# A new order of issue for the first nine slots of a sparse attention with a folded feed-forward

## The chip, the cores and the metric

One NeuronCore of a Trainium2 chip. The metric is the device time of one execution in microseconds; before the change three runs gave a median of 270.12 us (268.2 to 274.05).

## The reference

```python
# q, k, v: (8, 8, 576, 64) float32
rel = pos[:, None] - pos[None, :]
mask_local   = (rel >= 0) & (rel < 32)                      # heads 0 to 3
mask_strided = (rel >= 0) & (pos[None, :] % 32 == pos[:, None] % 32)   # heads 4 to 7
scores = np.where(masks, q @ k.T / sqrt(64), -1e9)
attn = softmax(scores) @ v
x = attn.transpose(0, 2, 1, 3).reshape(4608, 512)
# feed-forward: w1, w2 (512, 1024), w3 (1024, 1024), w_out (1024, 512)
out = ((x @ w1) * (x @ w2)) @ w3 @ w_out
```

## The kernel before, in words

The heads are taken two at a time. A "pair" i is one batch element and two heads: there are 32 pairs, four to a batch element, of which the first two (i % 4 of 0 and 1) have the local mask and the other two the strided one. The sparse masks let scores be computed in small blocks: nine 64-wide blocks for a local pair, eleven residue groups of 54 for a strided one.

The steps of a pair, each a helper of its own:

- `load_qk` and `load_v`: q and k come through POOL's DMA queue and are converted to 16 bit on the way. v of a strided pair does so too, in four transfers (L130); v of a local pair comes in 32 bit through SP's queue (L117, L119).
- `emit_cast_v`, `shift_v`: for a local pair, v is converted on a compute engine (L281) and a copy that is shifted by 32 rows is made by two DMAs of SP's queue (L289, L290).
- `emit_T`: q and k are transposed on PE (L301) into PSUM, and copied out (L309 on ACT or DVE for local pairs, L314 on DVE and L315 on ACT for strided ones). There are two PSUM buffers of this kind, shared with `emit_P`.
- `emit_S`: the scores on PE (L333 local, L339 strided) and on DVE the addition of the mask (L345).
- `emit_max`, `emit_sub` on DVE (L353, L360), `emit_exp` on ACT (L372).
- `emit_norm`: sum and reciprocal on DVE (L380, L382), and the multiplication (L383) on POOL or, where the call says so, on DVE.
- `emit_P`: the weights are transposed on PE (L401) and copied out (L404).
- `emit_V`: the products with v on PE (L421 local, L438 strided), copied into the four xT tiles.

In parallel w3 and w_out are folded into one 1024 x 512 matrix, wfh. w3 is loaded in four quarters (`load_w3(c, 2)` with c = 0, 2, 4, 6 brings rows c and c + 1), w_out in two halves (`load_wo`). `fold_t(mc)` transposes one of eight row blocks of w3 on PE (L223, copied out by L225), and `fold_m(mc, half)` multiplies it with half of w_out (four matmuls of L233; the second half ends with a copy, L236). w1 and w2 come in two halves each (`load_w`, L205).

The feed-forward is a row of pieces, handed out by `feed(us, batches)`: it emits pieces until their costs (0.87 us for an x @ w1 or x @ w2 piece, four matmuls of L248 or L258; 1.74 for an output piece, L269) have used up the credit given. Six PSUM buffers are shared by scores, folds, products with v and the feed-forward.

The order on each engine is the order in which these helpers are called. For slots 0 to 8 the calls are written out by hand, and from slot 9 on a loop issues them in a regular pattern. Engines wait for each other by semaphores that the framework sets from the data and the buffers. Every queue is in order, so a transfer that stands behind a waiting POOL instruction waits with it. In the built program a DMA of POOL waits on one of eight counters, which the DMA eight places before it used too.

Of the kernel before, what the change touches and what calls it, by code (L numbers as in the profile page):

```python
# [27 lines left out]
def kernel(  # L28
# [11 lines left out]
    nc = tc.nc  # L40
# [47 lines left out]
    def load_qk(i, which="qk"):  # L88

        b, hp, local, par = where(i)  # L90
        h0 = 2 * hp
        t = cast.get(i)
        if t is None:
            t = cast[i] = ld.tile([P, 2, ST * D], FP16, tag="s16", bufs=4, name="s16")
        if i + 1 == 4 * B:
            for p0 in (0, HALF):
                nc.vector.memset(t[p0 + 32:p0 + HALF, 1, (ST - 1) * D:ST * D], 0.0)
        for src, p0 in [((q, 0), (k, HALF))["qk".index(c)] for c in which]:
            if local:
                nc.gpsimd.dma_start(t[p0:p0 + HALF, :, 0:LB * D],  # L100
                                    src[b, h0:h0 + 2].rearrange("h (p j) d -> p h (j d)", j=LB))
            else:
                for h in range(2):
                    for r0, ap, n in strided_rows(i, h, ST):
                        nc.gpsimd.dma_start(t[p0 + r0[0]:p0 + r0[1], h, 0:n * D],  # L105
                                            _ap(src[b, h0 + h], 0 + ap[0], ap[1] + [[1, n * D]]))
# [100 lines left out]
    def load_wo(c):  # L207
        nc.gpsimd.dma_start(woh[:, c:c + 4, :], wor[:, c:c + 4, :])

    def load_w3(c, n=2):  # L210
        w3 = wst.tile([P, n, DF], FP16, tag="w3s", bufs=4, name="w3s")
        nc.gpsimd.dma_start(w3.rearrange("p i n -> p (i n)"), w3r[:, c // 2, :])
        for i in range(n):
            w3st[c + i] = w3[:, i, :]
# [62 lines left out]
    def emit_cast_v(i, eng=nc.gpsimd.tensor_copy):  # L277
        b, hp, local, par = where(i)
        if local:
            vst = staged.pop(i)  # L280
            eng(out=vhL[par][:, 1], in_=vst)  # L281
            pts.setdefault(i, {})["v"] = vhL[par]
# [208 lines left out]
    def zero_S():  # L491
        for t in qTS + prS:
            nc.vector.memset(t, 0.0)

    def zero_L(i):
        nc.vector.memset(kTL[i][:, 0:QB], 0.0)
        nc.vector.memset(vsL[i][HALF:P, LC - 1], 0.0)
        nc.vector.memset(vhL[i][0:QB, 0, 0], 0.0)
        nc.vector.memset(prL[i][:, LB, :], 0.0)

    dve = nc.vector
    cp, act, pool = nc.vector.tensor_copy, nc.scalar.copy, nc.gpsimd.tensor_copy
    with tc.manual_schedule():
        zero_S()
        load_qk(1, "q")
        zero_L(1)
        load_qk(0, "q")
        load_qk(1, "k")
        load_v(1)
        load_qk(0, "k")  # L510
        load_qk(2, "k")
        emit_cast_v(1, cp)
        load_w3(2, 2)
        make_identity(nc, id16)
        make_maskL()
        zero_L(0)
        load_qk(2, "q")
        emit_T(0)
        load_w3(4, 2)
        emit_T(1)  # L520
        make_sel()
        load_wo(0)
        make_maskS()
        emit_S(0)
        load_qk(3, "q")
        fold_t(2, act)
        emit_max(0)
        emit_sub(0)
        emit_S(1)
        load_qk(3, "k")  # L530
        emit_T(2)
        emit_exp(0)
        fold_t(3, act)
        load_wo(4)
        load_v(0, True)
        fold_t(4, act)
        emit_max(1)
        fold_t(5, cp)
        emit_S(2)
        fold_m(5, 0)  # L540
        load_v(2)
        fold_m(3, 0)
        emit_sub(1)
        emit_exp(1)
        emit_norm(0, dve)
        load_w3(6, 2)
        load_qk(4, "k")
        fold_m(4, 0)
        load_qk(4, "q")
        emit_max(2)  # L550
        load_qk(5, "k")
        emit_norm(1)
        fold_m(2, 0)
        emit_T(3)
        emit_sub(2)
        emit_S(3)
        load_qk(5, "q")
        emit_max(3)
        fold_m(5, 1)
        fold_m(4, 1, cp)  # L560
        emit_exp(2)
        fold_m(3, 1, cp)
        emit_sub(3)
        emit_P(1, cp)
        fold_m(2, 1)
        fold_t(6, act)
        load_w3(0, 2)
        fold_t(7, cp)
        emit_T(4, cp)
        emit_exp(3)  # L570
        emit_norm(2, dve)
        fold_m(6, 0)
        emit_S(4)
        emit_max(4)
        emit_cast_v(0, act)
        load_qk(6, "q")
        emit_sub(4)
        load_qk(6, "k")
        emit_T(5)
        fold_m(7, 0)  # L580
        fold_m(7, 1)
        emit_P(2)
        emit_P(0, cp)
        load_qk(7, "k")
        load_w(w1r, w1h, 0)
        emit_S(5)
        load_qk(7, "q")
        fold_t(0, act)
        fold_t(1, cp)
        emit_T(6)  # L590
        load_v(3)
        emit_max(5)
        load_w(w2r, w2h, 0)
        fold_m(1, 0)
        emit_norm(3)
        shift_v(0)
        emit_exp(4)
        emit_sub(5)
        emit_exp(5)
        fold_m(1, 1, cp)  # L600
        fold_m(0, 0)
        emit_norm(4)
        fold_m(6, 1)
        emit_P(3)
        shift_v(1)
        load_w(w1r, w1h, 1)
        fold_m(0, 1)
        emit_V(0)
        emit_norm(5)
        emit_S(6)  # L610
        emit_T(7)
        emit_max(6)
        emit_V(1)
        emit_V(2)
        load_w(w2r, w2h, 1)
        emit_V(3)
        load_v(4, True)
        emit_P(4)
        emit_P(5)
        emit_sub(6)  # L620
        load_v(5, True)
        emit_exp(6)
        emit_S(7)
        feed(0.65, 1)
        feed(1.67, 1)
        emit_max(7)
        emit_norm(6)
        feed(0.54, 1)
        load_qk(8, "q")
        load_qk(8, "k")  # L630
        feed(0.90, 1)
        feed(2.64, 1)
        emit_P(6, cp)
        feed(0.53, 1)
        feed(1.52, 1)
        emit_cast_v(4, act)
        shift_v(4)
        load_qk(9, "q")
        load_v(6)
        emit_cast_v(5, act)  # L640
        feed(0.11, 1)
        shift_v(5)
        emit_sub(7)
        load_qk(9, "k")
        emit_exp(7)
        emit_norm(7, dve)
        feed(1.96, 1)
        feed(0.98, 1)
        load_v(7)
        load_qk(11, "q")  # L650
        emit_T(8)
        feed(0.65, 1)
        feed(0.65, 1)
        load_v(8)
        load_qk(10, "q")
        load_v(9, True)
        load_qk(13, "k")
        feed(0.65, 1)
        emit_S(8)
        emit_V(4, cp)  # L660
        emit_cast_v(8, act)
        feed(0.30, 1)
        emit_T(9, cp)
        load_qk(10, "k")
        load_v(10)
        emit_V(5, cp)
        emit_V(6)
        load_qk(12, "q")
        feed(0.65, 1)
        shift_v(8)  # L670
        emit_max(8)
        load_qk(11, "k")
        emit_sub(8)
        feed(1.34, 1)
        emit_exp(8)
        emit_norm(8)
        load_qk(13, "q")
        emit_P(7)
        feed(1.33, 1)
        emit_cast_v(9, cp)  # L680
        load_qk(12, "k")
        feed(0.20, 1)
        feed(1.58, 1)
        for n in range(9, NP + 2):
            full = (n - 1) // 4
            first = full - 1 if n % 4 == 1 else full
            f = 5.2
            if n < NP:
                shift_v(n)
                emit_S(n)  # L690
            if n + 1 < NP:
                emit_T(n + 1)
            if n + 5 < NP:
                load_qk(n + 5)
            for i in (n + 3, n + 2):
                if i < NP and where(i)[2] == (i == n + 3):
                    load_v(i)
            for i in (n - 3, n - 2):
                if i + (3 if by_dma(i) and i % 4 < 3 else 2) == n:
                    emit_V(i)  # L700
            if n < NP:
                emit_max(n)
            feed(0.1 * f, first)
            if n < NP:
                emit_sub(n)
                emit_exp(n)
                emit_norm(n)
                if n + 1 < NP:
                    emit_cast_v(n + 1)
            feed(0.15 * f, first)  # L710
            if n <= NP and not by_dma(n - 1):
                emit_P(n - 1)
            feed(0.55 * f, full)
            if n < NP and n % 2 == 1:
                for i in (n - 1, n):
                    if by_dma(i):
                        emit_P(i)
            feed(0.2 * f, full)
        feed(1e9, B)
# [31 lines left out]
```

## Time and profile before

| | |
|---|---|
| median of three runs | 270.12 us (268.2, 274.05, 270.12) |
| the profiled execution | 271.13 us, span 269.4 us |
| PE busy | 251.3 us, 93% of the span |
| DVE, ACT, POOL busy | 176.0, 140.7, 152.8 us |
| DMA | 38.75 MB, mean 144 GB/s |
| first transpose of q and k (L301) | 6.53 us |
| first matmul of the fold (L233) | 19.14 us |
| first feed-forward product (L248) | 46.50 us |

The span runs from the first to the last instruction of the core; the execution's own time is 1.7 us longer. Where PE's busy share is near 100% the time is set by PE; elsewhere the row "idle before" of an instruction and its releaser tell what PE waited for. DMA rates count the bytes as they were written, in 16 bit for what was converted on the way.

### The profile page before, as it was taken

To read this page: it belongs to the slowest core of one execution; us is meant where nothing else is said; L and a number is where in the kernel's file an instruction comes from. 1 tells how busy PE (TensorE), PEld (TensorE's weight loads), DVE (VectorE), ACT (ScalarE), POOL (GpSimd) and SP (SyncE) were. 2 spreads that over 40 slices of the span, in tenths; PEclk is the share of its full clock that TensorE was granted. 3 is DMA by queue.
4 is the path that set the end of the run, shared out by engine and by line. 5 is a ranking of instruction groups with operands and counts; after the bars stand their busy time and mean duration, and the time that the engine had idled before them with its cause. 6 is when DMAs were issued, how large, how long until landed. Compare 5 with 4: busy or idle time off the path is not lost. (4 is left out here: it accounts for less than half of the span.)

```text
span 269.4 us, 9826 instructions
## 1 busy us (share of the span) xinstructions
PE 251.3 (93%) x4186; PEld 131.2 (49%) x4186; DVE 176.0 (65%) x353; ACT 140.7 (52%) x256; POOL 152.8 (57%) x236
## 2 busy tenths in 40 slices
PE   0588997999999999999999999999999999999995
PEld 0464655445554555554555455544454444444443
DVE  2379997677778777868886787678768823432210
ACT  1563767565754664666566456545655444333322
POOL 8757776398984895489568846885684110000000
PEclk9999999999999999999999999999999999999999
DMA  7999999999999699699999997996688142001113
GB/s 118 192 198 208 185 198 147 174 162 205 225 199 186 107 227 202 98 193 176 175 110 228 190 144 70 259 179 97 52 210 102 30 105 82 2 0 76 42 58 141
DMA packets 66238, 38.75 MB, mean 144 GB/s; under 512 B 45589, under 2 KB 60945, under 8 KB 66193
## 3 DMA queue, kind: packets, MB, share of 16 engines
q0 software_dynamic: 22112, 17.29, 43.0%
q1 hardware_dynamic: 44080, 20.82, 37.8%
q8 instruction: 33, 0.54, 0.8%
q14 instruction: 13, 0.10, 0.1%
HBM read 39.24 MB, written 9.44 MB: 181 GB/s over the span
## 5 line engine op out<-in xcount | busy, mean ns | idle before, releaser
L248 PE MATMUL aps<-xT,w1h 128*128 128x512 f16 x288 | 74.1, 380 | 0.0
L258 PE MATMUL bps<-xT,w2h 128*128 128x512 f16 x288 | 73.9, 379 | 0.0
L261 DVE TENSOR_TENSOR abt<-bps,asb 128x512 f16<-128x512 f32 x72 | 47.7, 678 | 33.1 <-PE bps L258 29.6
L269 PE MATMUL ops<-wfh,abt 128*128 128x512 f16 (+1 forms) x296 | 65.6, 374 | 0.0
L252 ACT COPY asb<-aps 128x512 f32<-128x512 f32 x72 | 41.4, 586 | 33.3 <-PE aps L248 20.2
L258 PEld LDWEIGHTS <-w2h 128*128 128x128 f16 x288 | 28.2, 98 | 34.0
L130 POOL DMA_DIRECT2D vhS<-in_v_dram x70 | 42.5, 719 | 3.8 <-DMA woh<-in_moe_w_out_dram 2.2
L269 PEld LDWEIGHTS <-abt 128*128 128x128 f16 x296 | 27.8, 98 | 30.3
L248 PEld LDWEIGHTS <-w1h 128*128 128x128 f16 x288 | 27.0, 98 | 30.7
L383 POOL TENSOR_TENSOR prS<-prS,rc 128x594 f16<-128x594 f16 x14 | 16.8, 1202 | 38.0 <-DVE rc L382 16.0
L274 ACT COPY osb<-ops 128x512 f32<-128x512 f32 (+1 forms) x36 | 20.7, 578 | 29.2 <-PE ops L269 24.2
L360 DVE TENSOR_TENSOR tmp<-tmp,mx 128x576 f32<-128x576 f32 (+1 forms) x32 | 25.7, 804 | 0.9
L353 DVE TENSOR_REDUCE mx<-tmp 128x9 f32<-128x576 f32 (+1 forms) x32 | 24.2, 758 | 0.5
L105 POOL DMA_DIRECT2D s<-in_q_dram x35 | 21.0, 631 | 6.0 <-PE tpk L301 2.1
L301 PE MATMUL tpq<-id,s 54*64 54x54 f16 (+1 forms) x640 | 17.6, 196 | 7.2 <-DMA s<-in_q_dram 6.5
L105 POOL DMA_DIRECT2D s<-in_k_dram x35 | 21.6, 679 | 2.0 <-DMA s<-in_q_dram 1.6
L372 ACT ACTIVATE prS<-tmp 128x594 f16<-128x594 f32 x16 | 11.2, 702 | 19.6 <-DVE tmp L360 12.4
L383 POOL TENSOR_TENSOR prL<-prL,rc 128x576 f16<-128x576 f16 x15 | 18.4, 1224 | 5.4 <-ACT osb L274 4.0
L301 PEld LDWEIGHTS <-s 54*64 54x64 f16 (+1 forms) x1280 | 14.7, 111 | 11.6 <-DMA s<-in_q_dram 6.5
L301 PE MATMUL tpk<-id,s 54*64 54x54 f16 (+1 forms) x640 | 17.4, 196 | 2.3 <-DMA s<-in_k_dram 2.0
L380 DVE TENSOR_REDUCE sm<-prS 128x11 f32<-128x594 f16 x16 | 12.3, 770 | 10.6 <-ACT prS L372 10.6
L380 DVE TENSOR_REDUCE sm<-prL 128x9 f32<-128x576 f16 x16 | 12.0, 749 | 10.9 <-ACT prL L372 10.9
(78 smaller groups left out, 271.5 us busy)
## 6 DMA issues: line engine op xcount, KB each, us to landing
out_dram<-osb SPq DMA_DIRECT2D x35, 256.0 KB, 2.8
vsL<-in_v_dram SPq DMA_DIRECT2D x32, 128.0 KB, 5.2
s<-in_q_dram POOLq DMA_DIRECT2D x16, 144.0 KB, 4.3
s<-in_k_dram POOLq DMA_DIRECT2D x16, 144.0 KB
s<-in_k_dram POOLq DMA_DIRECT2D x31, 74.2 KB, 5.1
s<-in_q_dram POOLq DMA_DIRECT2D x31, 74.2 KB, 5.7
w3s<-in_moe_w_dram POOLq DMA_DIRECT2D x4, 512.0 KB, 7.0
vhL<-vhL SPq DMA_DIRECT2D x16, 120.0 KB, 4.6
```

The costliest lines, as they stand in the source:

```text
L105: nc.gpsimd.dma_start(t[p0 + r0[0]:p0 + r0[1], h, 0:n * D], _ap(src[b, h0 + h], 0 + ap[0], ap[1] + [[1, n * D]]))
L130: nc.gpsimd.dma_start(vt[HALF * half + r0[0]:HALF * half + r0[1], h, 0:m * D], _ap(v[b, h0 + h], 6 * half * D + ap[0], ap[1] + [[1, m * D]]))
L248: nc.tensor.matmul(aps, cols(w1h, ci, jc), xT[ci][:, c * NT:(c + 1) * NT], start=(ci == 0), stop=(ci == KC1 - 1))
L252: nc.scalar.copy(out=asb, in_=aps)
L258: nc.tensor.matmul(bps, cols(w2h, ci, jc), xT[ci][:, c * NT:(c + 1) * NT], start=(ci == 0), stop=(ci == KC1 - 1))
L261: nc.vector.tensor_mul(abts[c][:, jc, :], bps, abts.pop((c, jc)))
L269: nc.tensor.matmul(ps, abts[c][:, jc, ts * P:(ts + 1) * P], wfh[:, jc, n * w:n * w + w], start=(jc == 0), stop=(jc == KC2 - 1))
L301: nc.tensor.transpose(tp[HALF * h:HALF * h + HALF, s, :], s16[p0:p0 + npar, h, s * D:(s + 1) * D], id16[p0:p0 + npar, p0:p0 + npar])
L353: nc.vector.tensor_reduce(out=mx, in_=tmp, axis=AX.X, op=ALU.max)
L360: nc.vector.tensor_tensor(out=tmp, in0=tmp, in1=_sub(mx, 0, P, 0, [[1, nt], [0, w]]), op=ALU.subtract)
L380: nc.vector.tensor_reduce(out=sm, in_=prv, axis=AX.X, op=ALU.add)
L383: eng.tensor_tensor(out=prv, in0=prv, in1=_sub(rc, 0, P, 0, [[1, nt], [0, w]]), op=ALU.mult)
```

## The change

Only the hand-written list of calls is edited; no helper is. In the list of slots 0 to 8 the loads of q and k of pairs 0 and 1 stand first, w3's third quarter (rows 4 and 5) is loaded and folded first, S(0) follows T(0) and S(1) follows T(1) with no fold between, and V(0) to V(3) stand shortly before the first `feed`. Some calls change their engine: the multiplication of `emit_norm(0)` goes from DVE to POOL and that of `emit_norm(3)` from POOL to DVE; conversions of v go from DVE to POOL (pairs 1 and 9), from ACT to POOL (pair 5) and from ACT to DVE (pairs 4 and 8); some copies out of PSUM change between ACT and DVE. One memset (`wz`, a tile that nothing reads) is added. The credits of the `feed` calls sum to 18.85 in both lists. The new list up to the first `feed`, two calls to a line in places, and then the cuts around the later ones:

```python
zero_L(0); load_qk(0, "q"); zero_S()
load_qk(1, "k"); load_qk(1, "q"); make_identity(nc, id16); load_qk(0, "k")
nc.vector.memset(wz, 0.0)
load_w3(4, 2); make_maskL()
emit_T(0); load_qk(2, "k"); emit_S(0); load_qk(3, "k"); load_qk(2, "q"); load_v(1)
zero_L(1); emit_T(1); emit_S(1)
load_w3(2, 2); emit_max(0); emit_max(1); make_sel(); load_wo(0); load_qk(3, "q")
fold_t(4, act); emit_sub(1); load_qk(4, "k"); load_v(0, True); load_wo(4); emit_cast_v(1)
fold_t(5, act); emit_T(2); load_w3(6, 2); fold_t(2, act); make_maskS(); emit_sub(0)
fold_t(3, cp); load_qk(5, "q"); emit_exp(1); emit_norm(1)
fold_m(5, 0); emit_exp(0); emit_T(3); emit_S(2); load_qk(4, "q")
fold_m(2, 0); emit_S(3); load_v(2); emit_max(2); emit_norm(0); emit_sub(2); emit_exp(2)
fold_m(4, 0); fold_m(3, 0); fold_m(2, 1, cp); fold_m(5, 1)
emit_P(1, cp); emit_P(0, cp); fold_m(3, 1, cp); load_qk(5, "k")
fold_m(4, 1); fold_t(6, act); emit_norm(2, dve); emit_T(4, cp); fold_t(7, cp)
emit_max(3); fold_m(6, 0); emit_T(5); emit_S(4); load_w3(0, 2); emit_P(2, cp); fold_m(7, 0)
load_qk(6, "k"); emit_sub(3); load_qk(6, "q"); shift_v(1); emit_cast_v(0, act); shift_v(0)
load_qk(7, "q"); emit_max(4); load_w(w1r, w1h, 0); emit_exp(3); load_qk(7, "k"); emit_sub(4)
load_v(3); fold_t(1, act); fold_t(0, act); load_w(w2r, w2h, 0); fold_m(7, 1)
emit_exp(4); emit_S(5); emit_max(5); emit_T(6); load_v(5, True); fold_m(6, 1)
emit_sub(5); emit_norm(3, dve); fold_m(0, 0); emit_exp(5); emit_norm(5)
load_w(w1r, w1h, 1); emit_norm(4); load_w(w2r, w2h, 1); fold_m(0, 1); fold_m(1, 0)
emit_S(6); emit_V(0); emit_P(3); fold_m(1, 1, cp); emit_V(1); emit_T(7); emit_V(2); emit_V(3)
emit_max(6); emit_sub(6); emit_S(7); emit_P(5)
feed(0.65, 1); feed(0.20, 1); emit_P(4, cp); emit_cast_v(5); feed(0.65, 1); emit_exp(6)
...
feed(1.08, 1); emit_T(8, cp); feed(2.64, 1); emit_S(8)
...
emit_norm(8); load_qk(12, "k"); load_qk(13, "q"); feed(1.67, 1); emit_cast_v(9); feed(1.51, 1)
```

More of the change, by code (lines that the diff above doesn't have):

```diff
@@ L503 @@
     with tc.manual_schedule():
+        zero_L(0)
+        load_qk(0, "q")
         zero_S()
+        load_qk(1, "k")
         load_qk(1, "q")
-        zero_L(1)
[L507 to L512, printed above, removed]
-        load_w3(2, 2)
[L514 to L520, printed above, removed]
+        make_identity(nc, id16)
@@ L521 @@
+        load_qk(0, "k")
+        nc.vector.memset(wz, 0.0)
+        load_w3(4, 2)
+        make_maskL()
+        emit_T(0)
+        load_qk(2, "k")
+        emit_S(0)
+        load_qk(3, "k")
+        load_qk(2, "q")
+        load_v(1)
+        zero_L(1)
+        emit_T(1)
+        emit_S(1)
+        load_w3(2, 2)
+        emit_max(0)
+        emit_max(1)
         make_sel()
         load_wo(0)
+        load_qk(3, "q")
+        fold_t(4, act)
+        emit_sub(1)
+        load_qk(4, "k")
+        load_v(0, True)
@@ L523 @@
+        load_wo(4)
+        emit_cast_v(1)
+        fold_t(5, act)
+        emit_T(2)
+        load_w3(6, 2)
+        fold_t(2, act)
         make_maskS()
[L524 to L527, printed above, removed]
         emit_sub(0)
-        emit_S(1)
-        load_qk(3, "k")
-        emit_T(2)
-        emit_exp(0)
[L533 to L538, printed above, removed]
+        fold_t(3, cp)
@@ L539 @@
+        load_qk(5, "q")
+        emit_exp(1)
+        emit_norm(1)
+        fold_m(5, 0)
+        emit_exp(0)
+        emit_T(3)
         emit_S(2)
-        fold_m(5, 0)
+        load_qk(4, "q")
+        fold_m(2, 0)
+        emit_S(3)
         load_v(2)
-        fold_m(3, 0)
[L543 to L550, printed above, removed]
-        load_qk(5, "k")
-        emit_norm(1)
@@ L553 @@
[L553 to L557, printed above, removed]
-        emit_max(3)
[L559 to L562, printed above, removed]
-        emit_sub(3)
[L564 to L569, printed above, removed]
-        emit_exp(3)
[L571 to L575, printed above, removed]
@@ L576 @@
-        load_qk(6, "q")
+        emit_max(2)
+        emit_norm(0)
+        emit_sub(2)
+        emit_exp(2)
+        fold_m(4, 0)
+        fold_m(3, 0)
+        fold_m(2, 1, cp)
+        fold_m(5, 1)
+        emit_P(1, cp)
+        emit_P(0, cp)
+        fold_m(3, 1, cp)
+        load_qk(5, "k")
+        fold_m(4, 1)
+        fold_t(6, act)
+        emit_norm(2, dve)
+        emit_T(4, cp)
+        fold_t(7, cp)
+        emit_max(3)
+        fold_m(6, 0)
+        emit_T(5)
+        emit_S(4)
+        load_w3(0, 2)
@@ L577 @@
+        emit_P(2, cp)
+        fold_m(7, 0)
+        load_qk(6, "k")
+        emit_sub(3)
+        load_qk(6, "q")
+        shift_v(1)
+        emit_cast_v(0, act)
+        shift_v(0)
+        load_qk(7, "q")
+        emit_max(4)
+        load_w(w1r, w1h, 0)
+        emit_exp(3)
+        load_qk(7, "k")
         emit_sub(4)
-        load_qk(6, "k")
-        emit_T(5)
-        fold_m(7, 0)
+        load_v(3)
+        fold_t(1, act)
+        fold_t(0, act)
+        load_w(w2r, w2h, 0)
         fold_m(7, 1)
-        emit_P(2)
@@ L583 @@
-        emit_P(0, cp)
-        load_qk(7, "k")
-        load_w(w1r, w1h, 0)
+        emit_exp(4)
         emit_S(5)
-        load_qk(7, "q")
-        fold_t(0, act)
-        fold_t(1, cp)
+        emit_max(5)
         emit_T(6)
-        load_v(3)
-        emit_max(5)
-        load_w(w2r, w2h, 0)
-        fold_m(1, 0)
[L595 to L599, printed above, removed]
-        fold_m(1, 1, cp)
-        fold_m(0, 0)
-        emit_norm(4)
-        fold_m(6, 1)
@@ L604 @@
[L604 to L610, printed above, removed]
+        load_v(5, True)
+        fold_m(6, 1)
+        emit_sub(5)
+        emit_norm(3, dve)
+        fold_m(0, 0)
+        emit_exp(5)
+        emit_norm(5)
+        load_w(w1r, w1h, 1)
+        emit_norm(4)
+        load_w(w2r, w2h, 1)
+        fold_m(0, 1)
+        fold_m(1, 0)
+        emit_S(6)
+        emit_V(0)
+        emit_P(3)
+        fold_m(1, 1, cp)
@@ L611 @@
+        emit_V(1)
         emit_T(7)
+        emit_V(2)
+        emit_V(3)
         emit_max(6)
[L613 to L618, printed above, removed]
-        emit_P(5)
-        emit_sub(6)
-        load_v(5, True)
-        emit_exp(6)
[L623 to L629, printed above, removed]
+        emit_sub(6)
+        emit_S(7)
@@ L630 @@
+        emit_P(5)
+        feed(0.65, 1)
+        feed(0.20, 1)
+        emit_P(4, cp)
+        emit_cast_v(5)
+        feed(0.65, 1)
+        emit_exp(6)
         load_qk(8, "k")
         feed(0.90, 1)
-        feed(2.64, 1)
-        emit_P(6, cp)
-        feed(0.53, 1)
         feed(1.52, 1)
[L636 to L644, printed above, removed]
@@ L645 @@
-        emit_exp(7)
-        emit_norm(7, dve)
+        emit_norm(6)
+        load_qk(8, "q")
+        load_v(4, True)
+        load_qk(10, "k")
         feed(1.96, 1)
         feed(0.98, 1)
-        load_v(7)
-        load_qk(11, "q")
[L651 to L666, printed above, removed]
+        feed(0.30, 1)
+        emit_max(7)
+        feed(0.53, 1)
+        emit_P(6)
+        load_qk(9, "k")
+        emit_sub(7)
+        emit_exp(7)
+        emit_cast_v(4, cp)
+        load_v(6)
+        shift_v(5)
+        load_qk(9, "q")
+        feed(0.90, 1)
+        shift_v(4)
+        feed(0.91, 1)
+        load_v(10)
+        load_qk(10, "q")
+        feed(1.08, 1)
+        emit_T(8, cp)
+        feed(2.64, 1)
@@ L667 @@
+        emit_S(8)
+        load_v(8)
+        emit_max(8)
+        load_v(7)
+        load_v(9)
+        emit_sub(8)
+        feed(0.65, 1)
+        load_qk(12, "q")
+        feed(0.54, 1)
+        emit_V(4, cp)
+        load_qk(13, "k")
+        emit_exp(8)
+        feed(1.15, 1)
+        emit_V(5)
+        emit_norm(7, dve)
+        emit_T(9, cp)
+        load_qk(11, "q")
         emit_V(6)
-        load_qk(12, "q")
-        feed(0.65, 1)
+        load_qk(11, "k")
+        feed(0.11, 1)
+        emit_cast_v(8, cp)
@@ L670 @@
+        emit_P(7, cp)
         shift_v(8)
[L671 to L675, printed above, removed]
         emit_norm(8)
+        load_qk(12, "k")
         load_qk(13, "q")
[L678 to L683, printed above, removed]
+        feed(1.67, 1)
+        emit_cast_v(9)
+        feed(1.51, 1)
         for n in range(9, NP + 2):
```

## The prediction

> **What bounds the kernel now.** I read the busy time by windows first. Columns: stretch, sum, PE, PEld, DVE, ACT, POOL, granted clock, DMA share, GB/s.
>
> ```profile
> 0.00:10.00 10.00, 0.95 (x36) 0.68 (x37) 2.63 (x13) 3.05 (x5) 8.49 (x22) 1.00 0.84 140
> 40.00:50.00 10.00, 8.42 (x245) 4.98 (x244) 7.26 (x20) 7.94 (x16) 4.57 (x5) 1.00 1.03 166
> 50.00:60.00 10.00, 10.00 (x86) 4.79 (x85) 6.98 (x13) 5.15 (x9) 8.47 (x15) 1.00 0.90 152
> 200.00:250.00 50.00, 49.96 (x422) 23.34 (x420) 23.57 (x42) 20.29 (x38) 7.20 (x10) 1.00 0.28 58
> ```
>
> From 50 us on PE is full and the edited slots hold the same instructions, so whatever the change does must show before the first feed-forward product at 46.50. PE's own list of waits says how much there is to win:
>
> ```profile
> PE tpq L301 <- DMA s<-in_q_dram: 6.5, 1, 6.5
> PE tpk L301 <- DMA s<-in_k_dram: 2.0, 1, 2.0
> PE op L421 <- issue: 1.5, 1, 1.5
> PE sp L339 <- ACT kT L315: 0.8, 1, 0.8
> PE w3tp L223 <- DMA w3s<-in_moe_w_dram: 0.7, 1, 0.7
> ```
>
> 8.5 us of these wait for the very first q and k, and about 5 us are all the others together. PE's timeline then gives the pace:
>
> ```profile
> 16.40 1.93 PE L223 MATMUL w3tp<-id,w3s 128*128 128x128 f16 x16 [0.66 <-DMA w3s<-in_moe_w_dram]
> 19.14 4.29 PE L233 MATMUL fps<-woh,w3T 128*128 128x512 f16 x16 [0.36 <-DMA woh<-in_moe_w_out_dram]
> 37.13 3.63 PE L233 MATMUL fps<-woh,w3T 128*128 128x512 f16 x16 [0.37 <-DVE w3T L225]
> 44.87 0.30 PE L421 MATMUL op<-pT,vhL 64*64 64x32 f16 x16 [1.53 <-issue]
> 46.50 1.04 PE L248 MATMUL aps<-xT,w1h 128*128 128x512 f16 x4
> ```
>
> The fold waits for w3 and w_out, and PE runs at half pace until about 20.5: the fold's matmuls start 0.427 us apart until 20.4 and 0.216 apart after (the granted clock reads 1.00 in both). The last view is POOL's timeline, since POOL issues all weight, q and k transfers in order:
>
> ```profile
> 20.52 0.59 POOL L212 DMA_DIRECT2D w3s<-in_moe_w_dram  x1
> 23.72 0.58 POOL L100 DMA_DIRECT2D s<-in_k_dram  x1 [1.39 <-DMA woh<-in_moe_w_out_dram]
> 24.37 1.74 POOL L383 TENSOR_TENSOR prL<-prL,rc 128x576 f16<-128x576 f16 x1
> 37.07 0.99 POOL L205 DMA_DIRECT2D w2h<-in_moe_w_dram  x1
> 39.27 1.49 POOL L383 TENSOR_TENSOR prS<-prS,rc 128x594 f16<-128x594 f16 x1 [1.20 <-DVE rc L382]
> 42.49 0.82 POOL L205 DMA_DIRECT2D w1h<-in_moe_w_dram  x1
> ```
>
> Two things are seen. A POOL transfer waits until the one eight places before it has landed (the waits in the program's list show the eight counters; the 1.39 us is such a wait). And a normalisation on POOL (L383) holds every transfer behind it: between 38.06 and 42.49 no issue left POOL. The semaphore stamps of the trace give landings: k of pair 0 at 8.76, w_out's first half 19.10, its second 23.19, w3's fourth quarter 27.50, k of pair 5 29.48, w3's first quarter 33.28, w2's first half 44.54. That is some 177 KB per us from 8.76 to 19.10 (1832 KB), so the transfers run end to end.
>
> **The change part by part.** I put both orders against the clock at points where PE has done the same work.
>
> *To the first pair.* q0, k1, q1 and now the identity (0.36 + 0.29 on POOL) stand ahead of k0, so k0 is issued 0.7 us later, at 4.0 instead of 3.28. The bytes ahead of it are the same, the shortest landing seen is 4.2 us after the issue, so it lands at the later of 8.2 and 8.8: no change. maskL is needed at 10.7 and, with POOL done at 6.7 and 1.3 us of ACT copies, ready at 8.3. The four memsets of zero_S (1.5 us), zero_L(0) and a memset of wz (0.3 us by the 0.36 us of a qTS memset) fall in DVE time that is empty until the first scores; that cover gone they would cost 2 us.
>
> *Score products directly behind their transposes.* S(0) now waits for ACT's copies of T(0) (0.64 + 0.65 us), S(1) for those of T(1); before, T(1) and the fold of w3 stood between. The chain is 8.8, T 0.7, copies to 10.7, S 0.67, T(1) 0.55, copies to 13.3, S(1) to 14.0. Before, S(1) ended at 13.9. No loss, but PE is idle for 2.5 us more and the fold it did there is still to do.
>
> *The fold.* Up to w_out's first half the queue now holds 148 KB more (k of pair 3): at 177 KB per us it lands 0.8 us later, 19.9. PE has by then done the four transposes of w3 (0.95 us each cold) and T(2), as before, but not S(2) (0.37). Then come the half folds (4 x 0.216 = 0.87, the first cold), T(3), S(2), S(3): 19.95 + 1.4 + 0.4 + 0.4 + 0.9 + 0.4 + 0.9 + 0.9 = 25.2. The same set was done at 25.0 before, which had lost 0.80 us to the kT copy. So +0.2.
>
> *From there to pair 5.* fold_m(2,1) and (5,1), P(1), then P(0), whose normalisation moves from DVE to POOL: S(3) ends at 23.4, DVE adds, maximum, sum and reciprocal (0.78 + 0.75 + 0.75 + 0.25) to 26.0, POOL to 27.3 (1.2 us as in most L383 rows). Behind it wait k of pair 5 and w3's first quarter: issued at 27.3 and 28.0 where they were at 23.72 and 26.69. Landings by the shortest 4.2 us and, for w3, another 2.8: 31.5 and 34.3. T(5) wants its k at 31.9 and fold_t(1) its w3 at 34.4. They are just in time; before, the quarter lay ready for 1.8 us. P(2) now follows T(5) in the two PSUM buffers and waits for the copy of qT, 0.5 us. Adding the remaining rows (eight half folds, two w3 transposes at 0.57, S 0.38, T 0.35) brings PE to 41.0 behind S(6).
>
> *The products with v at the end.* V(0) needs the shifted v; its conversion now stands on ACT behind pair 5's copies, at 34.1, against 32.3 before, and the shift took 7.2 us: 41.9, a wait of about 1 us. Then P(3), half a fold, V(1), T(7), V(2), V(3), to 45.4; S(7) must wait for kT of pair 7, behind two xT copies on ACT, to 45.95; S(7) and P(5) to 46.8. The first feed-forward product comes at 46.9, +0.4. P(4), 0.36 us, is still to come: +0.75 in all.
>
> *The 1.53 us in front of V(1).* The page names no releaser. It falls where some 350 very short PE instructions follow each other. The new order is as dense there. Bounds: 0, if it depends on the old order, and 1.5, if it comes again; I take half, 0.75, since nothing ranks the two.
>
> *Behind 46.9.* The pieces sum to 18.85 us of credit in both lists and PE was full; w1's and w2's second halves have 7 us to land, q of pair 8 lands by about 57 against a T(8) at 58. The conversion of v of pair 4 moves to DVE and may hold its products behind it for about 1 us, which six PSUM banks cover. Nothing added.
>
> Sum: +0.75 + 0.75 = +1.5. The profiled execution took 271.13 us (span 269.4), so 272.6 on its scale; it lies 1.0 us above the median of the three times shown, so I forecast 270.12 + 1.5 = 271.6.
>
> [...] The fold's first matmuls ran 0.427 us apart at 19.14 though PE had been transposing nearly without a gap from 11.35 to 15.5. [...]
>
> **The rivals.**
> *Slower: POOL starves the weights.* If the sum of pair 0 is ready 4 us later than I have it, because q of pair 3, S(3) and four DVE operations stand in one line before it, k5 and w3's first quarter leave 4 us later, and PE, which has 0.1 us of slack there, stops at T(5) and fold_t(1) for all of it: +1.5 + 4 = +5.5, 275.6. For it: a 4.4 us hole of the same kind at 38.06. Against it: there the waits had cover. It decides once k5 is issued after 28.
> *Faster: the pace doubles earlier.* If the unbroken run 13.35 to 16.65 lifts the pace, T(3) and the first half fold save 0.43 + 0.85, two w3 transposes 0.4 each, of which the last two are lost against w_out's landing; without the 1.53 us too the result is 1.5 - 0.75 - 1.3, less the wait at V(0) if the shift is quick: -1.5, 268.6. Against it: the same kind of run left the pace halved before. Even with no wait at all behind w_out's landing at 19.1, PE's rows (16 half folds 13.9, 0.9 for the slow first ones, some 9.5 for the short products) reach 43.4, so the gain can hardly pass 3.5 us.
> *Nothing changes.* The weights run end to end in both orders and set the start of the feed-forward (44.54 for w2): 270.1.
>
> **How the numbers follow.** Forecast 0.47, starved weights 0.28, earlier pace 0.15, nothing 0.10. About 2% (5.4 us) is what a measurement of this kernel can tell from no change. Faster by more needs more than PE's 3.5 us and so mostly luck in the runs: 0.07. Slower by more holds most of the starved case and the upper end of the forecast: 0.28. The rest, 0.65, is within. The range goes from 267.3 (the earlier pace and some) to 277.5 (the starved case with the 1.5 us again).
>
> **What would show it.** First feed-forward product (L248) at 46.9 to 47.7, against 46.50; S(0) and S(1) each behind an ACT copy by over 1 us; L233 first at about 19.9; POOL's second L383 from about 26 with a k transfer directly behind; PE waiting for vhL ahead of V(0). Wrong: a first L248 before 45 or after 50, waits of PE between 50 and 200 us, or an L233 pace that is still 0.427 after 23.

## The result, and the profile after

The new order takes 274.06 us (median of six runs, 272.01 to 274.54) against 270.25 us beside it: ratio 1.0118, 95% interval 1.0070 to 1.0166. By that ratio it is slower by some 3 us; the forecast was +1.5. The ratio compares fast runs alone, while the plain medians lie 3.8 us apart. The profiled execution took 273.7 us, span 272.0; its own run was 0.4 us below the median, that of before 0.9 above, so the spans differ by 2.6 us only.

The windows of the new order, columns as before:

```profile
0.00:10.00 10.00, 1.07 (x48) 0.90 (x52) 2.12 (x9) 3.73 (x6) 8.54 (x22) 1.00 0.85 153
40.00:50.00 10.00, 9.55 (x249) 5.59 (x247) 9.73 (x23) 7.73 (x16) 5.39 (x7) 1.00 1.04 177
50.00:60.00 10.00, 10.00 (x86) 4.75 (x84) 7.26 (x15) 5.03 (x8) 6.39 (x10) 1.00 1.02 171
200.00:250.00 50.00, 49.93 (x539) 23.91 (x527) 24.98 (x48) 21.10 (x40) 9.72 (x15) 1.00 0.28 64
```

PE is full from 50 us on, as before. Its waits:

```profile
PE tpq L301 <- DMA s<-in_q_dram: 5.3, 1, 5.3
PE sp L333 <- ACT kTL L309: 2.5, 2, 1.3
PE w3tp L223 <- DMA w3s<-in_moe_w_dram: 2.4, 1, 2.4
PE tpk L301 <- DMA s<-in_k_dram: 2.4, 1, 2.4
PE op L421 <- DMA pT<-prL: 1.0, 1, 1.0
PE pp L401 <- issue: 0.9, 1, 0.9
```

S(0) and S(1) now wait for ACT's copies (2.5 us together), and the transposes of w3 wait 2.4 us for w3's second quarter. PE's timeline shows what comes of it:

```profile
18.07 1.07 PE L223 MATMUL w3tp<-id,w3s 128*128 128x128 f16 x8 [2.38 <-DMA w3s<-in_moe_w_dram]
20.62 1.86 PE L233 MATMUL fps<-woh,w3T 128*128 128x512 f16 x4 [0.33 <-DMA woh<-in_moe_w_out_dram]
25.11 3.63 PE L233 MATMUL fps<-woh,w3T 128*128 128x512 f16 x16
47.75 1.03 PE L248 MATMUL aps<-xT,w1h 128*128 128x512 f16 x4
```

The first product with w_out starts at 20.62 instead of 19.14, and the first feed-forward product at 47.75 instead of 46.50, with P(4) still to do. From the one to the other it took 27.1 us, 27.4 before (of which 1.53 are the wait in front of V(1)): once the fold has begun, the two heads are about equally long. So 1.25 of the 2.6 us between the two spans lie ahead of the first L248. Behind it the new order is longer too in this profile: P(4), forecast at 0.36 us, is still to come, and the waits of 1.0 and 0.9 us in the list stand there. The first question is why the fold began 1.5 us late. Windows of the same kind, from 12 to 16 and from 28 to 32 us, first before, then the new order (the last two columns are DMA share and GB/s):

```profile
12.00:16.00 4.00, 3.67 (x111) 2.93 (x98) 3.64 (x9) 2.81 (x6) 3.85 (x8) 1.00 1.03 198
28.00:32.00 4.00, 3.80 (x113) 2.52 (x114) 3.61 (x6) 3.06 (x5) 3.56 (x6) 1.00 1.09 196
```

```profile
12.00:16.00 4.00, 3.25 (x96) 2.85 (x95) 2.81 (x5) 2.24 (x4) 3.56 (x6) 1.00 0.92 132
28.00:32.00 4.00, 3.59 (x30) 2.12 (x28) 3.17 (x6) 1.54 (x3) 4.00 (x6) 1.00 0.74 108
```

There are two dents. In the first, ahead of w3's second quarter and w_out, the rate is 132 GB/s for 198; the mean 4 KB packet took 0.37 to 0.62 us in each microsecond of it, against 0.33 to 0.34 in the same stretch of before. In the second, near 29 us, the queue is short of transfers. By the semaphore stamps w3's second quarter landed at 18.02 and w_out's first half at 20.58 (19.10 before).

### The profile page after: what moved, and what is told of

The parts are those of the page before. It is cut to its first block, busy times and chain, and to the rows that moved or that the text cites. A ratio compares the mean times of both kernels' runs of the same rounds, so it can differ in the third digit from the quotient of the medians.

```text
span 272.0 us, 9825 instructions
## 1 busy us (share of the span) xinstructions
PE 252.1 (93%) x4186; PEld 131.2 (48%) x4186; DVE 176.6 (65%) x354; ACT 138.5 (51%) x252; POOL 154.9 (57%) x239
## 4 chain that ended last, share of the span: by engine, by line
PE 76%; DMA 8%; DVE 5%; POOL 5%; issue 2%; SPq 2%; ACT 2%; DVEq 0%; POOLq 0%; ACTq 0%
PE ops L269 22%; PE aps L248 20%; PE bps L258 20%; DMA woh<-in_moe_w_out_dram 3%; DMA pT<-prL 3%; PE fps L233 3%; PE tpq L301 3%; PE op L421 2%; POOL s L105 2%; PE sp L333 2%; DMA vhS<-in_v_dram 2%; DVE sm L380 1%; PE sp L339 1%; PE op L438 1%; PE pp L401 1%
## 5 line engine op out<-in xcount | busy, mean ns | idle before, releaser
L248 PE MATMUL aps<-xT,w1h 128*128 128x512 f16 x288 | 74.1, 380 | 0.0
L261 DVE TENSOR_TENSOR abt<-bps,asb 128x512 f16<-128x512 f32 x72 | 47.8, 679 | 31.9 <-PE bps L258 30.1
L248 PEld LDWEIGHTS <-w1h 128*128 128x128 f16 x288 | 27.1, 98 | 31.1
L274 ACT COPY osb<-ops 128x512 f32<-128x512 f32 (+1 forms) x36 | 20.7, 578 | 34.4 <-PE ops L269 31.7
L383 POOL TENSOR_TENSOR prS<-prS,rc 128x594 f16<-128x594 f16 x13 | 15.3, 1180 | 33.1 <-ACT asb L252 18.0
L383 POOL TENSOR_TENSOR prL<-prL,rc 128x576 f16<-128x576 f16 x16 | 19.6, 1226 | 12.6 <-ACT osb L274 4.6
L345 DVE TENSOR_TENSOR tmp<-sp,maskL 128x320 f32<-128x320 f32 (+1 forms) x32 | 13.1, 451 | 17.2 <-PE sp L333 17.2
L372 ACT ACTIVATE prS<-tmp 128x594 f16<-128x594 f32 x16 | 11.2, 700 | 21.8 <-DVE tmp L360 15.8
L380 DVE TENSOR_REDUCE sm<-prS 128x11 f32<-128x594 f16 x16 | 12.3, 769 | 9.7 <-ACT prS L372 9.7
```

Of the source, the lines that this page charges most:

```text
L248: nc.tensor.matmul(aps, cols(w1h, ci, jc), xT[ci][:, c * NT:(c + 1) * NT], start=(ci == 0), stop=(ci == KC1 - 1))
L261: nc.vector.tensor_mul(abts[c][:, jc, :], bps, abts.pop((c, jc)))
L274: (nc.vector.tensor_copy if last and n == 0 else nc.scalar.copy)(out=osb, in_=ps)
L383: eng.tensor_tensor(out=prv, in0=prv, in1=_sub(rc, 0, P, 0, [[1, nt], [0, w]]), op=ALU.mult)
```

## The experiments

The theory at first: the head makes the loss, by late data for the fold. Rivals: slots 6 to 8 make it; POOL's held queue does (the prediction's own rival); the half pace of TensorE does, which in the new order lasted until about 24.3 us. All ratios are to the kernel before, on the same chip. The table, for reference, has the landing of w_out's first half, the first L233 and the first L248, each from the one profiled execution of a kernel, and the ratio, from all its runs:

| kernel | w_out | L233 | L248 | ratio (95%) |
|---|---|---|---|---|
| before | 19.10 | 19.14 | 46.50 | 1 |
| new order | 20.58 | 20.62 | 47.75 | 1.0118 (1.0070 to 1.0166) |
| e1 no memset | 20.85 | 20.89 | 48.64 | 1.0120 (1.0072 to 1.0168) |
| e2 new head | 20.58 | 20.68 | 47.19 | 1.0185 (1.0135 to 1.0235) |
| e3 new tail | 19.16 | 19.36 | 46.50 | 1.0234 (1.0190 to 1.0278) |
| e4 w3 sooner | 20.11 | 20.18 | 46.62 | 1.0130 (1.0094 to 1.0165) |
| e5 norms back | 20.94 | 20.98 | 49.84 | 1.0095 (1.0058 to 1.0133) |
| e6 warm | 20.50 | 21.12 | 47.23 | 1.0108 (1.0062 to 1.0154) |
| e7 fold block | 22.00 | 22.05 | 51.65 | 1.0183 (1.0143 to 1.0223) |
| e9 old start | 18.73 | 18.85 | 45.87 | 1.0054 (1.0019 to 1.0089) |
| e10 new start | 21.18 | 21.23 | 48.14 | 1.0073 (1.0032 to 1.0114) |
| e11 k3 later | 18.87 | 18.91 | 45.74 | 1.0015 (0.9980 to 1.0050) |
| e12 old, k3 early | 20.00 | 20.18 | 47.35 | 1.0049 (1.0014 to 1.0083) |

**e1, the new order again.** `- nc.vector.memset(wz, 0.0)`

> The new order without the added memset of wz, which nothing reads. My theory (the loss is made before the first feed-forward product, because the second and third quarter of w3 and w_out's first half land late) and its rival (the loss is made behind it, in slots 6 to 8) both expect no change from the new order: 272 to 274.5 us, ratio to before 1.008 to 1.016. It serves as a second profile of the new order: if the slow transfer of w3's second quarter (5.3 us from the landing ahead of it, 2.6 for the same size before) belongs to the order, it comes again and the first product with w_out (L233) starts at 20.3 to 20.9; if it was an accident of one run, it lands by about 16 and L233 starts at 18.8 to 19.6.

1.0120: no cost of the memset can be told, and the late landings come again (w3's second quarter 17.52, w_out 20.85). The two waits of 0.9 and 1.0 us behind 50 us are not in this profile, so they do not come in every run. Its span is 0.9 us shorter than the new order's though its first L248 comes 0.9 us later. What share such waits have in the medians is not shown. Half pace lasted until about 27.0 here.

**e2 and e3, head and tail by themselves.** New list up to the first `feed` and the old one behind, and the reverse.

> The new order up to the first feed call, then v of pair 4, P(4) and exp(6), and from there the old order. The theory that the head makes the loss: first L248 at 47.7 to 48.2 (P(4) now stands ahead of it), 271.5 to 272.5 us, ratio 1.005 to 1.010. The rival that slots 6 to 8 make it: 270 to 271, ratio under 1.004.

> The old order up to the first feed call, and from there the new one. The theory that the head makes the loss: 270.5 to 271.5 us, ratio 1.001 to 1.005, for the 0.9 us wait ahead of P(7) and perhaps the 1.0 us wait for a transposed pT near 111. The rival that slots 6 to 8 make it: 272.5 to 274, ratio 1.008 to 1.014.

The new head with the old tail loses all of it by its ratio (1.0185), more than either expectation. Its profile does not show where: that execution was the fastest of the six (271.03 us, their median 273.95), its span is 269.3 us, as before, and its first L248 is 0.7 us later than before. One profile of a kernel is one run of several that lie up to 5 us apart. e3 missed both expectations and does not price the new tail, for the combination made a wait of its own:

```profile
54.97 0.71 POOL L281 CAST vhL<-vsL 128x640 f16<-128x640 f32 x1 [8.90 <-DMA vsL<-in_v_dram]
55.63 0.62 POOL L100 DMA_DIRECT2D s<-in_k_dram  x1
56.27 1.20 POOL L383 TENSOR_TENSOR prS<-prS,rc 128x594 f16<-128x594 f16 x1
```

The new tail converts v of pair 5 on POOL, and the old head loads that v late; the conversion holds POOL 8.9 us, the normalisation of pair 6 behind it too, and PE waits 3.1 us at P(6) for that. In the profile, again the fastest of six, this is nearly all of the 3.3 us by which the span is longer than before. The ratio stands for some 6 us, so the other half is not explained, and e3 does not refute the rival that slots 6 to 8 cost time.

**e4, w3's second quarter sooner.** `load_w3(2, 2)` goes from behind `emit_S(1)` to behind `emit_T(0)`.

> The new order with the load of w3's second quarter directly behind maskL, ahead of k and q of pairs 2 and 3. The theory that its late landing costs the head: fold_t(2) no longer waits 2.4 us, w3's quarter lands at about 13, T(2) waits for its q until about 15.4, w_out's first half comes as late as by the bytes ahead of it (19.9, or 18 to 19 if the slow stretch goes away); L233 first at 19 to 20, 0.5 to 1.5 us faster than the new order, ratio to before 1.003 to 1.010. The rival that the start of the fold is covered later by waits for data: no change, 1.012.

The quarter landed at 14.71 and fold_t(2) no longer waited for it, but T(2), ahead of it on PE, waited for its q instead, and w_out came at 20.11. No gain (1.0130), though w_out came 0.5 us and the first L248 1.1 us sooner than in the new order. That speaks against a theory in which the first L248 alone sets the time; what this kernel lost instead is not shown. Which quarter of w3 comes when made no difference that can be told.

**e5, the normalisations back on their engines.** `emit_norm(0)` to `emit_norm(0, dve)`, `emit_norm(3, dve)` to `emit_norm(3)`.

> The new order with the two normalisations on their old engines: emit_norm(0) on DVE, emit_norm(3) on POOL. The theory of the held queue (the 1.5 us multiplication on POOL and its 1.7 us wait for the sum hold k of pair 5 and w3's first quarter, and the transfers pause near 29 us): the pause goes away, k5 is issued at about 26.5 instead of 29.3, P(0) no longer waits 0.4 us, first L248 at 46.5 to 47.2, 1 to 2 us faster than the new order, ratio to before 1.004 to 1.009. The theory of the pace (the head is slow because TensorE stays at half pace until 22.6 to 26.8, against 20.5 to 21.9 in the old head) expects the pause to go away too, but at most 0.5 us of time: ratio 1.009 to 1.014.

1.0095, not to be told from the new order. (The granted clock was 0.98 in this profile, so only its transfers are read.) POOL's timeline tells why nothing was gained:

```profile
26.23 0.75 POOL L100 DMA_DIRECT2D s<-in_k_dram  x1
29.09 0.59 POOL L212 DMA_DIRECT2D w3s<-in_moe_w_dram  x1 [2.10 <-DMA w3s<-in_moe_w_dram]
```

k of pair 5 left 3.1 us sooner, as the held-queue theory had it. But w3's first quarter stands exactly eight transfers behind its fourth (q5, q4, four of v, k5 between them; five behind it in the old order), shares its counter and waited until that had landed, at 28.80. It landed at 35.66, 35.72 in the new order. The dent has two causes, one behind the other, and PE did not wait for either: fold_t(1) starts at 36.6.

**e6, more work for TensorE.** `warm(5)` ahead of `fold_t(2)`, `warm(3)` ahead of `fold_m(5, 0)`.

> The new order with eight matmuls more that nothing reads (128x512 of a zero tile): five ahead of fold_t(2), where PE idles 2 to 3 us, and three ahead of the first fold product. The theory of the pace: the matmul spacing halves by 18 to 21 us, the first fold products take 0.87 us, first L248 at 46 to 47, 1 to 2 us faster than the new order, ratio 1.004 to 1.009. The theory of the held queue, or of late data in general: no gain, ratio 1.010 to 1.014, or worse by the 0.7 us of the last three.

```profile
21.12 1.03 PE L233 MATMUL fps<-woh,w3T 128*128 128x512 f16 x4
22.44 0.36 PE L339 MATMUL sp<-kT,qTS 64*64 64x54 f16 x22
26.67 1.67 PE L233 MATMUL fps<-woh,w3T 128*128 128x512 f16 x7 [0.76 <-DMA woh<-in_moe_w_out_dram]
```

The pace is full from the first L233 (1.03 us for what took 1.86), and the time cannot be told from the new order's, 1.0108. Of what PE won it lost 0.76 us again to w_out's second half, which a slower PE had not waited for. By the interval, whose lower end is 1.0062, a gain of up to some 1.5 us is not excluded, but the pace does not make all of the loss.

**e7, the first half folds in one row.** S(2), `fold_m` (5,0), (3,0), (4,0), (2,0), then T(3), S(3).

> The new order with the first four half folds in one row, as in the old one: S(2), then fold_m(5,0), (3,0), (4,0), (2,0), then T(3) and S(3). The theory of the pace: sixteen L233 in a row double the pace within 1.3 to 3.4 us of their start, at 22 to 24 in every run, gain 0.5 to 1 us less what T(3) and with it pair 3 lose by coming 3.3 us later; ratio 1.007 to 1.012. The theory of the held queue: S(3) and thus the sum of pair 0 come 1 to 2 us later, k5 and w3's first quarter too, ratio 1.014 to 1.020.

1.0183. T(3) and S(3) come later, and with them the sum of pair 0 that POOL waits for:

```profile
31.50 1.49 POOL L383 TENSOR_TENSOR prL<-prL,rc 128x576 f16<-128x576 f16 x1 [5.67 <-DVE rc L382]
32.94 0.67 POOL L100 DMA_DIRECT2D s<-in_k_dram  x1
33.60 0.58 POOL L212 DMA_DIRECT2D w3s<-in_moe_w_dram  x1
```

w3's first quarter left at 33.6, where the new order had 29.98, and landed at 39.44; the first L248 comes at 51.65. But PE stops neither at T(5) nor at fold_t(1) here. It waits 2.1 us at P(0) for the multiplication itself, and 1.7 us at the start of the fold for w_out's first half, which landed at 22.00. So the queue can be held longer than in the new order, and the prediction's rival, a PE that stops for k of pair 5 or w3's first quarter, is still not seen. The sixteen L233s in a row took 5.11 us, for 3.63 at full pace; with the spacings of 0.427 and 0.216 us their pace doubled, by estimate, some 3.0 us after their start (by the same sum 1.3 us in before, whose sixteen took 4.29, and 3.4 in e12, 5.35).

**e8, more work in the old order.** 36 unread matmuls where PE idles.

> The old order with unread matmuls where PE idles: 24 ahead of T(0), four each ahead of fold_t(2), fold_t(4) and fold_m(5,0); the memset of their tile stands first. The theory of the pace, applied to the old order: T(0) to the fold run at full pace, the fold starts no sooner (w_out lands at 19.1) but its first products take 0.87 instead of 1.5 us; 0.5 to 1.5 us faster than before, ratio 0.994 to 0.998. The rival that the transfers alone set the head: 1.000, or up to 1.004 if the extra matmuls delay what they stand ahead of.

No price came of this: the granted clock was 0.976 in its profile and 0.976 to 0.988 in all runs but one, which fell to 0.654; the clock of before, on the same chip, was mostly 1.00, and one of its runs fell to 0.671.

**e9 and e10, split at the first fold product.** Old list up to `fold_m(5, 0)` and the new one behind, and the reverse.

> The old order up to the first fold product, fold_m(5,0); from there the new one (with the six calls that the new order had already made put directly behind it: k4, w3's fourth quarter, sub(1), exp(1), q5, norm(1)). The theory that the first 20 us make the loss (w_out's first half lands 1.0 to 1.7 us later in the new order, and the pace of TensorE doubles 1 to 6 us later): first L233 at 19.1 to 19.5, pace doubled by 22, 1.5 to 3 us faster than the new order, ratio to before 1.000 to 1.006. The rival that the stretch from 20 to 47 us makes it (transfers held by POOL and by the eight counters, products with v late): ratio 1.008 to 1.014.

> The new order up to fold_m(5,0), then exp(0) and S(2), and from there the old order. The theory that the first 20 us make the loss: first L233 at 20.5 to 21, ratio 1.007 to 1.013. The rival that the stretch behind makes it: 0.998 to 1.005.

With the old start the fold begins at 18.85 and the ratio falls to 1.0054, as the theory of the first 20 us had it; the new start by itself costs 0.73%, with w_out at 21.18. Each half holds some of the loss by its ratio, and the intervals overlap.

**e11, one load.** `load_qk(3, "k")` goes from between S(0) and q of pair 2 to behind `load_qk(3, "q")`, so behind w_out's first half; all else is the new order.

> The new order with k of pair 3 loaded behind w_out's first half, with its q. The theory that the bytes ahead of w_out (148 KB more than before, 0.8 us) cost time: w_out's first half at 19.7 to 20.1, first L233 0.6 to 1 us sooner than the 20.6 to 21.0 of the new order, 0.5 to 1 us faster, ratio 1.008 to 1.010. The rival that only the rate of the transfers between 12 and 17 us counts: w_out at 20.6 as before, ratio 1.010 to 1.014.

1.0015, interval 0.9980 to 1.0050: clear of the new order's (each against before on its own chip), and not to be told from before. More than either theory had it. The window from 12 to 16 us and PE's timeline:

```profile
12.00:16.00 4.00, 3.25 (x96) 2.86 (x95) 3.05 (x7) 2.24 (x4) 3.72 (x6) 1.00 1.07 210
```

```profile
18.91 1.87 PE L233 MATMUL fps<-woh,w3T 128*128 128x512 f16 x4 [0.36 <-DMA woh<-in_moe_w_out_dram]
45.74 1.03 PE L248 MATMUL aps<-xT,w1h 128*128 128x512 f16 x4
```

The rate is 210 GB/s again, w_out lands at 18.87 for 20.58, and the whole head moves with it: the first L248 comes 2.0 us sooner. S(0) and S(1) still wait their 2.5 us, k of pair 5 is still behind a normalisation, and half pace still lasts past 21.8: none of these makes the loss by itself.

The move changes more than the 148 KB. It takes 1.1 us of issuing off POOL ahead of w3's second quarter (issued at 8.52 for 9.61), and it makes w_out's first half the 11th of POOL's transfers instead of the 13th. As the 13th it stands exactly eight behind w3's third quarter, the 5th, and shares its counter. First e1, which has the load order of the new one, then e11:

```profile
13.04 0.56 POOL L208 DMA_DIRECT2D woh<-in_moe_w_out_dram  x1 [1.60 <-DMA w3s<-in_moe_w_dram]
```

```profile
10.27 0.56 POOL L208 DMA_DIRECT2D woh<-in_moe_w_out_dram  x1
```

Seven kernels have the new load order up to w_out. In five of them (e1, e2, e6, e7, e10) POOL waited 1.2 to 1.8 us at this place until w3's third quarter had landed, at 12.3 to 12.9. In the profiles of the new order and of e5 the quarter landed at 10.3 and 11.1, nothing waited, and the rate fell instead, to 153 and 160 GB/s from 12 to 18 us. So e11 shows that this one load in its place makes the loss, but not by which of the three ways.

**e12, the reverse in the old order.** `load_qk(3, "k")` ahead of `load_qk(2, "q")`.

> The old order with one move, the reverse of the one that took the loss out of the new order: k of pair 3 is loaded ahead of q of pair 2 and so ahead of w3's third quarter and w_out's first half. The theory that this load in this place is the loss (148 KB, and a lower rate of the transfers behind six small ones): w_out's first half lands at 20.2 to 21.2 instead of 19.1, first L233 there too, 1.5 to 2.5 us slower than before, ratio 1.006 to 1.010. If only the bytes count, 19.9 to 20.0 and ratio 1.002 to 1.004. The rival that w_out's landing has cover in the old order (its fold needs w3's quarters first and PE runs slowly there): no change, 0.998 to 1.002.

w_out landed at 20.00, as the bytes alone had it (19.9 to 20.0), first L248 0.85 us later, ratio 1.0049 (1.0014 to 1.0083). The one load is a loss in the old order as well, though a smaller one. w_out's first half is the 13th transfer here too, but the 5th is one of k of pair 2, which had landed at 8.89, and POOL did not wait. So the bytes and their issuing moved w_out by 0.9 us; what the new order lost beyond that did not come with them.

## Why the prediction was right or wrong, point by point

The main mechanism, that k of pair 3 ahead of w_out delays the fold, was right, and its size was off: of some 3 us the sum had 1.5. Half of that 1.5 was taken for a wait in front of V(1) that did not come, so the head's share was 0.75, and that the total came as near as it did is in part luck.

- *To the first pair, no change*: no loss, as forecast, and a small gain that nothing kept. k of pair 0 landed at 7.91, not at 8.8, T(0) began at 7.96 and S(1) was done at 13.1 for 14.0, but the fold behind them waits for its data; no cost of the memset can be told (e1). The 4.2 us were not the shortest landing in the trace: q of pair 8 took 3.0 (issued at 52.65, landed at 55.64).
- *Score products behind their transposes, no loss*: right. The waits are there, 1.23 and 1.26 us, and e11 has them too without losing time.
- *The fold, w_out 0.8 us later*: this is the term that was mis-sized. The prediction saw the cause, 148 KB of k of pair 3 ahead of w_out, and charged the bytes alone, at the rate of before, 177 KB per us. For the bytes that was about right: in e12, where the load is early too but POOL does not wait ahead of w_out, it is 0.9 us. The new order's transfers from k0 (7.91) to w_out (20.58) ran at 1980 KB / 12.67 us = 156. So w_out came 1.5 us late in that profile, and 1.4 to 2.9 us late in the seven kernels that keep this load order (the new order, e1, e2, e5, e6, e7, e10: 20.50 to 22.00). The prediction had named the counter that a transfer shares with the one eight places before it, but did not count out w_out's new place, where e1, e2, e6, e7 and e10 waited 1.2 to 1.8 us.
- *From L233 to L248*: 19.95 to 46.9 was forecast, 27.0 us; measured 27.1. That they agree is luck: two errors cancel. The fold up to fold_m(3,0) with T(3), S(2) and S(3) took 6.2 us for 5.3, as half pace lasted longer, and the wait of about 1 us forecast ahead of V(0) did not come, since PE reached it just as v landed (43.39 and 43.34). P(2) waited 0.4 for the copy of qT, as forecast; P(0) waited 0.4 too, which the sum did not have.
- *The 1.53 us in front of V(1)*, taken at half: not in the head of the new order. A wait of the same unnamed kind, 0.9 us, stood at P(7) near 69, and e1's profile has neither. Its price is not settled.
- *Nothing behind 46.9*: not settled either. e9, with the old start and the new rest, is 0.5% slower than before, and e11, with the same rest, 0.15%, though the first L248 of both profiles comes 0.6 to 0.8 us sooner than before. So the rest seems to cost something, from the first L248 on 0.9 to 1.4 us more than before in the profiles of the new order, e9 and e11 (P(4) among it), but e1's profile has 0.4 us less than before there. A part of this may be the spread of single runs.
- *The starved queue*: its late issues did occur, k5 at 29.3 and w3's first quarter at 29.98, later than the 27.3 and 28.0 of the sum and past the 28 that the rival named as its point, but without a stop of PE at T(5) or fold_t(1), since PE came some 2 us later too (T(5) at 34.2 for 31.9, fold_t(1) at 36.6 for 34.4). A part of that dent was overlooked: the quarter's counter (e5).
- *The earlier pace*: it went the other way, to 24.3 and 27.0 for 20.5, and e6 shows no cost of this that can be told. That an unbroken run of PE lifts the pace was this rival's assumption and is not shown: in the new order PE worked nearly without a gap from 12.44 to about 15.7, stood for 2.38 us ahead of fold_t(2), and the first four L233s, from 20.62, still took 1.86 us for the 1.03 of full pace. The stretch of before from 11.35 to 15.5 that the prediction calls transposing holds two sets of score products as well (0.67 us each), so it does not show what transposes by themselves do to the pace. Nor did half pace end at one time in all profiles: the new order and e1, which differ by one memset, have 24.3 and 27.0, and the eleven profiles whose L233s show the doubling have it between 20.0 and 27.0 us.
- *Nothing changes, since w2 sets the start*: wrong. w2's half landed at 47.02 and was first used at 48.90.
- *The signs*: S(0) and S(1) behind ACT's copies, and k of pair 5 directly behind POOL's second L383 (at 27.9 for 26), came as forecast. The first L248 at 47.75 lies just past the stretch named, and no wait for v stood ahead of V(0). Two of the three signs that the prediction itself calls wrong did appear: L233s 0.42 us apart after 23 (up to 24.3, in e1 up to 27.0), and waits of PE between 50 and 200 us (0.9 and 1.0).

What stays open is why the rate dips, and what share the bytes, the issuing and the shared counter have in the loss. Over 12 to 18 us eight of the nine orders with k of pair 3 early had 153 to 182 GB/s (the new order 153, e1 180, e2 175, e5 160, e6 175, e7 166, e10 182, e12 178), those without it 188 to 201 (before 194, e3 188, e9 201, e11 200). The ninth, e4, had 194: there w3's second quarter stands ahead of the six transfers of 74 KB. So the dip goes with these six directly ahead of two of 512 KB; whether their number, their place or the late issue behind them makes it was not tried. Nor was a kernel that only takes the counter away. And the first L248 does not tell the time of a kernel by itself (e2, e4): that the one load makes the loss rests on the ratios of e11 and e12.

## What to carry to other kernels

Where the transfers run end to end at the start, the first large operand that the long chain needs comes no sooner than the queue ahead of it (in before 1832 KB in 10.3 us, and w_out's first half at 19.10): count what stands there, and move out what is used later, here one k that was wanted 2 us after w_out. An order on PE that looks worse (2.5 us of idle waits for copies) can be free behind that landing, as in e11 (ratio 1.0015), and a faster PE may buy the next wait for data, as in e6 (0.76 us). Charge such bytes at a measured rate (177 KB per us here), and then count how many places apart two large transfers stand when issues are counted by a fixed number of counters, here eight: w3's quarter eight places ahead of w_out held its issue for up to 1.8 us. Profile a kernel more than once before reading a difference of 1 us from it.

## What was not expected of the hardware

TensorE's half pace did not end at a fixed time: 20.5 us before, 24.3 in the new order and 27.0 in e1, which differs from it by one memset. The order of PE's work alone does not explain it: e2, e4 and e11 also have the first products with w_out four at a time among transposes, and their pace doubled at 21.8, 20.7 and 21.9. With five unread matmuls of 0.427 us ahead of the transposes and three ahead of the products (e6) it had doubled by 20.6. Thirty-six of them in the old order went along with a granted clock of 0.976 and a span of 281.0 us.
